# Attention by four-head groups with sinks padded to full tiles, between the matmuls of a token and channel mixer

## The chip, the cores and the metric

The kernel runs on one core of one Trainium2 chip. The metric is the device time of one execution in microseconds (us). Executions are sorted into fast and slow by their time (slow: over 1.5% above the fastest run of the same kernel). Medians and extremes that are quoted are of all runs, and the text says where slow ones are among them. The engines are called as in the profile: PE (TensorE matmuls), PEld (its weight loads), ACT (ScalarE), DVE (VectorE), POOL (GpSimd) and SP (SyncE, which here only issues DMAs).

## The reference, cut to what matters

Attention with 4 batches, 8 heads, 768 positions and 64 columns per head: each query sees a window of 128 keys and the first 4 keys ("sinks"). The heads are put side by side to x (4 x 768 x 512), which goes through an MLP mixer.

```python
keep = is_sink | ((rel >= 0) & (rel < window))          # n_sink = 4, window = 128
a = softmax(where(keep, q @ k.T / 8, -1e9)); x = heads_side_by_side(a @ v)
u = x + (relu(x.T @ w_tok1) @ w_tok2).T                 # 768 -> 256 -> 768
out = u + relu(u @ w_ch1) @ w_ch2                       # 512 -> 1536 -> 512
```

Inputs and output are fp32; both kernels compute in bf16.

## The kernel before: the parts that count

Two heads (one "pair") lie side by side in the 128 partitions, 64 rows each. A tile scheduler orders each engine's instructions. Scores are computed transposed (keys on partitions), one matmul of 64 rows at a time, each with its own exp on ACT and its own mask multiply on DVE or POOL. P·V (the exponentials of the scores, times the values) takes, for each head and query tile, the current key tile, the previous one, and the sinks, which are a matmul of **4 rows**.

```python
# loads: casting DMAs (fp32 in, bf16 out) of POOL's queue, six for each pair
nc.gpsimd.dma_start(out=qk_bf[:, 0, :, i], in_=q[b, h0 + i].rearrange("(t p) d -> p t d", p=P))
# scores
nc.tensor.matmul(ps_s[:, 0:nq * P], kT[:, kt], qT[:, kt:kt + nq], start=True, stop=True)       # 64 rows
nc.scalar.activation(pT[:, kt, i, 0:nq], ps_s[:, 0:nq * P], AF.Exp, scale=scale)
eng.tensor_tensor(out=pT[:, kt, i, 0:nq], in0=pT[:, kt, i, 0:nq], in1=msk[:, i, 0:nq], op=ALU.mult)
# ... sink scores
nc.tensor.matmul(ps_sk, kT2[ds(64 * i, 64), 0, 0:4], qT2[ds(64 * i, 64), 2:NT], start=True, stop=True)
# P.V of one head and one query tile
nc.tensor.matmul(ps_o, pT[:, qt, i, 0], vh[:, qt], start=True, stop=(qt == 0))                 # L149
nc.tensor.matmul(ps_o, pT[:, qt - 1, i, 1], vh[:, qt - 1], start=False, stop=(qt == 1))        # L151
nc.tensor.matmul(ps_o, pT_sink[:, i, ts(qt - 2, P)], vh[0:4, 0], start=False, stop=True)       # L153, 4 rows
# ... mixer of one batch: token product (L171, L182), transposes, channel products (L199, L208)
```

The mixer of batch b is spread between the attention of batch b+1.

The softmax here doesn't subtract the row's maximum and nothing guards it: scores larger than these inputs give would overflow.

## Time and profile before

Median 330.11 us (325.12 to 332.06, 4 runs, of which 331.77 and 332.06 are slow by the 1.5% rule); the profiled run spans 326.6 us.

The page of the kernel before, first its line of busy times (share of the span, instructions), then three of its lines of 40 equal slices of 8.2 us: the busy tenths of PE, the granted TensorE clock, and the busy tenths of the DMA engines.

```profile
PE 289.8 (89%) x1743; PEld 140.8 (43%) x1760; DVE 137.3 (42%) x491; ACT 164.2 (50%) x441; POOL 150.7 (46%) x215
...
PE   1584299899999999999999999999999999889994
...
PEclk9999999999999998999999999999959999999999
DMA  9999999999395773528379095313000002100022
```

PE is the busiest engine, and from 40 us on it is nearly always busy. What it is busy with is the question. The timeline of PE (start, duration in us, engine, line, operation, output and inputs, rows\*columns of the stationary operand, which PEld loads, then rows x columns of the moving one; the rows of both are the contraction rows, over which the matmul sums):

```profile
231.22 0.20 PE L149 MATMUL ps_o<-v_aug,pT 128*128 128x65 bf16 x1
231.26 0.20 PE L151 MATMUL ps_o<-v_aug,pT 128*128 128x65 bf16 x1
231.39 0.20 PE L153 MATMUL ps_o<-v_aug,pT_sink 4*128 4x65 bf16 x1
231.52 0.20 PE L149 MATMUL ps_o<-v_aug,pT 128*128 128x65 bf16 x1
...
232.46 0.34 PE L199 MATMUL ps_mx<-uT,w_ch_96 128*128 128x384 bf16 x1
232.73 0.28 PE L123 MATMUL ps_sc<-qT_2966,kT_2967 64*128 64x256 bf16 x1
232.94 0.20 PE L149 MATMUL ps_o<-v_aug,pT 128*128 128x65 bf16 x1
```

Matmuls overlap, so their durations are not to be added: read the distance from start to start. L149 to L151, both of 128 rows, is 0.04 us; L151 to L153, from 128 rows to 4, is 0.13 us, and so is the way back. A 384-column matmul that is followed by another of its kind takes 0.162 us (median of all in the trace); before a matmul of 64 rows it takes 0.27. Each change of the number of contraction rows costs about 0.1 us. Counted through all PE matmuls in order of time, there are 551 such changes.

The table of stages (start:end, length, then busy us and number of instructions of each engine, granted clock, share of DMA, which adds up the packets' times and can exceed 1, GB/s) has as its borders the first matmul of each batch's mixer. The first stage is the attention of batch 0 alone, three stages mix batch b's mixer with batch b+1's attention, and the last is the last mixer alone.

```profile
0.00:66.90 66.90, 41.30 (x238) 19.51 (x239) 24.57 (x103) 33.33 (x91) 54.62 (x81) 1.00 1.23 116
66.90:145.40 78.50, 76.31 (x463) 36.87 (x467) 37.10 (x136) 42.51 (x120) 43.22 (x59) 0.98 0.67 58
145.40:213.80 68.40, 67.14 (x438) 33.19 (x441) 34.79 (x123) 40.32 (x110) 36.28 (x50) 1.00 0.61 59
213.80:280.60 66.80, 65.41 (x401) 31.75 (x403) 30.12 (x112) 35.09 (x95) 14.38 (x22) 0.95 0.11 27
280.60:327.00 46.40, 39.67 (x214) 19.44 (x215) 10.69 (x19) 12.98 (x26) 2.18 (x4) 1.00 0.11 40
```

The mixed batches are bound by PE: the second busiest engine, ACT, has 40 of 68 us. The first of them is 10 us longer than the next. Its matmuls tell why; the timeline at the first mixer:

```profile
66.93 1.46 PE L171 MATMUL ps_mx<-x_sb_98,w_tok_94 128*128 128x512 bf16 x3
```

Three matmuls of 512 columns start 0.40 to 0.43 us apart; after 88 us the same shape steps 0.216 us. Two rows of another matmul of 512 columns, on either side of 88 us:

```profile
85.98 1.06 PE L182 MATMUL ps_mx<-h1T,w_tok_95 128*128 128x512 bf16 x2
...
88.81 0.59 PE L182 MATMUL ps_mx<-h1T,w_tok_95 128*128 128x512 bf16 x2
```

PE runs at half clock until then. The line PEclk does not show it: the first clock record of the packed trace begins at 87.6 us (no view prints it), and where there is no record the line shows full clock. Two shorter stretches at half clock are on record, 3.4 us from 128.6 us and 6.8 us from 237.8 us.

### The profile page before, as it was taken

The numbers are of one execution on the slowest core, as the hardware profiler recorded it, in microseconds if no ns is written. First come the engines' busy times: TensorE is split into PE (matmuls) and PEld (weight loads), VectorE is DVE, ScalarE is ACT, GpSimd is POOL, SyncE is SP. The second block draws the span as 40 slices with busy tenths as digits, with TensorE's granted clock in tenths as the row PEclk, the third lists the DMA queues.
The fourth block names the chain that finished last, engine by engine and source line by source line (L and its number), as shares of the span: only waits on it lengthen the run. The fifth ranks groups of instructions, "written<-read, shape, count | busy, mean of one in ns | idle before, by whom it ended". The sixth has DMA issues, their size and how long they took to land.

```text
span 326.6 us, 4967 instructions
## 1 busy us (share of the span) xinstructions
PE 289.8 (89%) x1743; PEld 140.8 (43%) x1760; DVE 137.3 (42%) x491; ACT 164.2 (50%) x441; POOL 150.7 (46%) x215
## 2 busy tenths in 40 slices
PE   1584299899999999999999999999999999889994
PEld 1221244333455554444545544444544454345541
DVE  1342155635763525237853335258614242350021
ACT  1374167756367887018378774063768730137400
POOL 8986559988375774217477455043223100000001
PEclk9999999999999998999999999999959999999999
DMA  9999999999395773528379095313000002100022
GB/s 71 90 183 206 173 64 73 76 58 72 26 61 38 50 49 25 88 101 78 24 54 71 3 61 66 101 63 27 0 2 0 1 19 101 75 2 0 2 96 96
DMA packets 82072, 19.98 MB, mean 61 GB/s; under 512 B 75808, under 2 KB 79136, under 8 KB 82048
## 3 DMA queue, kind: packets, MB, share of 16 engines
q0 software_dynamic: 79024, 15.34, 54.2%
q1 hardware_dynamic: 1728, 2.36, 1.9%
q10 hardware_dynamic: 1296, 1.97, 1.6%
q8 instruction: 14, 0.23, 0.3%
q14 instruction: 10, 0.08, 0.1%
HBM read 26.74 MB, written 6.29 MB: 101 GB/s over the span
## 4 chain that ended last, share of the span: by engine, by line
PE 54%; issue 22%; POOL 8%; DMA 7%; DVE 4%; ACT 4%; POOLq 0%; ACTq 0%
PE ps_mx L199 14%; PE ps_mx L208 10%; PE ps_sc L123 9%; DMA qk_bf<-in_k_dram 6%; PE ps_o L149 5%; PE ps_o L153 4%; PE ps_mx L171 3%; DVE u_sb L186 2%; POOL qk_bf L94 2%; POOL pT L131 2%; PE ps_sc L138 2%; PE ps_tr L108 2%; ACT pT L127 2%; PE ps_mx L182 1%; PE ps_tr L107 1%
## 5 line engine op out<-in xcount | busy, mean ns | idle before, releaser
L127 ACT ACTIVATE pT<-ps_sc 128x256 bf16<-128x256 f32 x192 | 66.5, 368 | 30.2 <-PE ps_sc L123 26.2
L199 PE MATMUL ps_mx<-uT,w_ch_96 128*128 128x384 bf16 x384 | 80.6, 332 | 0.7 <-DVE uT L190 0.5
L208 PE MATMUL ps_mx<-w_ch_97,v1T 128*128 128x512 bf16 x278 | 67.1, 384 | 0.4
L203 ACT ACTIVATE v1T<-ps_mx 128x384 bf16<-128x384 f32 x96 | 46.6, 489 | 35.0 <-PE ps_mx L199 34.8
L131 POOL TENSOR_TENSOR pT<-pT,mask_main 128x256 bf16<-128x256 bf16 (+1 forms) x80 | 50.2, 634 | 23.9 <-ACT pT L127 21.8
L154 DVE RECIPROCAL recip<-ps_o 128x1 f32<-128x1 f32 x192 | 29.8, 164 | 66.8 <-PE ps_o L153 40.7
L199 PEld LDWEIGHTS <-w_ch_96 128*128 128x128 bf16 x384 | 35.0, 98 | 25.5 <-issue 6.6
L222 POOL DMA_DIRECT2D out_dram<-o_sb x7 | 4.0, 574 | 81.8 <-DVE o_sb L213 81.8
L208 PEld LDWEIGHTS <-v1T 128*128 128x128 bf16 x288 | 27.6, 98 | 32.1 <-issue 1.8
L213 DVE TENSOR_TENSOR o_sb<-ps_mx,u_sb 128x512 f32<-128x512 f32 x24 | 16.6, 691 | 58.6 <-PE ps_mx L208 58.6
L149 PE MATMUL ps_o<-v_aug,pT 128*128 128x65 bf16 x192 | 37.1, 212 | 3.1 <-DVE x_sb_98 L160 1.1
L98 POOL DMA_DIRECT2D v_aug<-in_v_dram x32 | 27.4, 861 | 22.8 <-PE ps_tr L107 7.8
L131 DVE TENSOR_TENSOR pT<-pT,mask_main 128x256 bf16<-128x256 bf16 (+1 forms) x80 | 34.4, 431 | 7.9 <-ACT pT L127 7.4
L94 POOL DMA_DIRECT2D qk_bf<-in_q_dram x32 | 27.4, 859 | 17.4 <-PE ps_o L149 7.1
L107 PE MATMUL ps_tr<-ident,qk_bf 128*128 128x128 bf16 x96 | 15.2, 257 | 20.1 <-DMA qk_bf<-in_q_dram 12.9
L151 PE MATMUL ps_o<-v_aug,pT 128*128 128x65 bf16 x160 | 32.6, 211 | 0.0
L149 PEld LDWEIGHTS <-pT 128*128 128x128 bf16 x192 | 18.6, 102 | 24.3 <-issue 11.6
L96 POOL DMA_DIRECT2D qk_bf<-in_k_dram x32 | 27.2, 859 | 0.2 <-issue 0.2
L153 PE MATMUL ps_o<-v_aug,pT_sink 4*128 4x65 bf16 x128 | 26.8, 209 | 0.0
L131 POOL TENSOR_TENSOR pT<-pT,mask_first 128x256 bf16<-128x256 bf16 x16 | 11.0, 686 | 19.9 <-ACT pT L127 19.9
L139 ACT ACTIVATE pT_sink<-ps_sc 4x512 bf16<-4x512 f32 x32 | 17.9, 582 | 4.4 <-PE ps_sc L138 4.0
L107 PEld LDWEIGHTS <-qk_bf 128*128 128x128 bf16 x96 | 8.8, 110 | 23.0 <-issue 12.2
(142 smaller groups left out, 313.9 us busy)
## 6 DMA issues: line engine op xcount, KB each, us to landing
qk_bf<-in_q_dram POOLq DMA_DIRECT2D x32, 96.0 KB, 3.1
qk_bf<-in_k_dram POOLq DMA_DIRECT2D x32, 96.0 KB, 3.3
v_aug<-in_v_dram POOLq DMA_DIRECT2D x32, 96.0 KB, 3.4
out_dram<-o_sb SPq DMA_DIRECT2D x8, 256.0 KB, 2.0
out_dram<-o_sb ACTq DMA_DIRECT2D x7, 256.0 KB, 2.0
out_dram<-o_sb POOLq DMA_DIRECT2D x7, 256.0 KB, 2.3
w_ch_96<-in_moe_w_ch_dram POOLq DMA_DIRECT2D x1, 1536.0 KB, 12.5
w_ch_97<-in_moe_w_ch_dram POOLq DMA_DIRECT2D x1, 1536.0 KB, 15.1
```

The lines of the kernel that those rows point to most:

```text
L94: nc.gpsimd.dma_start(out=qk_bf[:, 0, :, i], in_=q[b, h0 + i].rearrange("(t p) d -> p t d", p=P))
L98: nc.gpsimd.dma_start(out=v_aug[:, i, :, 0:D], in_=v[b, h0 + i].rearrange("(t p) d -> p t d", p=P))
L123: nc.tensor.matmul(ps_s[:, 0:nq * P], kT[:, kt], qT[:, kt:kt + nq], start=True, stop=True,)
L127: nc.scalar.activation(pT[:, kt, i, 0:nq], ps_s[:, 0:nq * P], AF.Exp, scale=scale,)
L131: eng.tensor_tensor(out=pT[:, kt, i, 0:nq], in0=pT[:, kt, i, 0:nq], in1=msk[:, i, 0:nq], op=ALU.mult,)
L149: nc.tensor.matmul(ps_o, pT[:, qt, i, 0], vh[:, qt], start=True, stop=(qt == 0))
L151: nc.tensor.matmul(ps_o, pT[:, qt - 1, i, 1], vh[:, qt - 1], start=False, stop=(qt == 1))
L153: nc.tensor.matmul(ps_o, pT_sink[:, i, ts(qt - 2, P)], vh[0:4, 0], start=False, stop=True)
L154: nc.vector.reciprocal(recip[:, i], ps_o[:, D:D + 1])
L199: nc.tensor.matmul(ps_v1, w_ch1[:, ct, ts(ft, P)], uT[:, ct, ds(half * (S // 2), S // 2)], start=(ct == 0), stop=(ct == NC - 1),)
L203: nc.scalar.activation(v1T[:, ft, ds(half * (S // 2), S // 2)], ps_v1, AF.Relu)
L208: nc.tensor.matmul(ps_out, v1T[:, ft, ts(st, P)], w_ch2[:, ft], start=(ft == 0), stop=(ft == NF - 1),)
```

## The change

The intent: fewer and larger instructions. Four heads form a group. Scores come in units of four matmuls of 64 rows with one wide exp; masks become selects on POOL (instructions that zero what lies outside the window), but for the first tile; loads are plain fp32 DMAs of SP, cast on chip; the sink operands are padded to 128 rows, so that P·V has one sink matmul of 260 columns for four heads; and PE's order is set by hand, with the attention of batch b+1 spread between the pieces of batch b's mixer.

```diff
+        nc.sync.dma_start(out=q32.rearrange("p h t d -> p h (t d)"),
+                          in_=q[b, h0:h0 + GH].rearrange("h (p t) d -> p h (t d)", t=NT))
+        ...                                              # k alike, v in 256-byte pieces; casts on POOL
+        ps = ps_sc.tile([P, 2, 512], FP32, name="ps_s", tag="sc")
+        for kt in (2 * u, 2 * u + 1):
+            for i in range(2):
+                nc.tensor.matmul(ps[:, i, n:n + w], G.kT[j][ds(64 * i, 64), ts(kt, P)],
+                                 G.qT[j][ds(64 * i, 64), ds(kt * P, w)], start=True, stop=True)
+        nc.scalar.activation(pT[:, :, 512 * u:512 * u + n], ps[:, :, 0:n], AF.Exp, scale=scale)
-                    nc.tensor.matmul(ps_o, pT_sink[:, i, ts(qt - 2, P)], vh[0:4, 0], start=False, stop=True)
+                nc.tensor.matmul(ps, G.pk[:, ts(qt - 2, P)], vsink[:, g], ...)     # 128 rows, four heads
+    with tc.manual_schedule(engines={PE}):
+        ...
+            main = a + m + c1 + c2
+            fill = batch_attention(b + 1) if b + 1 < B else []
+            run(spread(main, fill, 0.05, 0.92))
```

## The prediction

> **What bounds the kernel now.** TensorE. On the page it is busy 89% of 326.6 us; ACT has 50%, POOL 46%, DVE 42%, and these overlap it. But much of that is not arithmetic:
>
> 1. *Tile-size switches.* In the timeline, successive 128-row 512- and 384-column matmuls start 216 and 162 ns apart. Where a 64-row score matmul follows they are 323 and 268 ns apart; a 65-column P·V matmul takes about 30 ns, but 129 ns before a 4-row sink matmul, and 131 ns after one. Each change of contraction rows thus costs about 105 ns. The Trainium skill, "TensorEngine Tiling (Array Packing)", Key Properties, says changing the tiling mode drains TensorE; this trace agrees and gives the size. I count 551 changes in the order of the matmuls: about 55 us.
> 2. *Half clock.* Until about 88 us a 512-column matmul steps 401 to 427 ns, then 216; the granted-clock line does not show it. "TensorE: Matmul & The Clock Gate", Part 1, has these two rates. From 40 to 88 us PE is busy, at half rate.
> 3. *Start.* 30–40 us is nearly empty: the chain of waits has 15.3 us for a k load behind the weight loads (casting DMAs). The first mixer matmul is at 67 us.
>
> **What the change does.**
> - Sinks: 128 four-row matmuls become 24 full-height ones of 260 columns, and score matmuls for sinks become full height. No 4-row switches remain.
> - Scores run in 48 units of four 64-row matmuls: about 96 switches, not 551. Saves about 48 us.
> - Fp32 loads by the SP queue, and casts on chip: POOL loses some 85 us of DMA issue (0.86 us each) and DMA work halves or better; it gains casts and masks (estimate from its 128x256 multiply, 0.68 us, and 128x128 select, 0.33 us: about 28 us per batch). ACT gets wide exps: by its 385 ns for 256 and 594 ns for 512 columns, 1.0 us for 1024; about 29 us per batch. DVE about 25 us.
> - PE order is fixed, so a late exp or mask now stalls everything behind it.
>
> **Sum (estimates from the steps above).** PE per mixer: 24 x 216 + 24 x 56 + 96 x 162 + 72 x 216 ns = 37.7 us. Attention per batch: transposes 2.7, scores with switches 5, sinks 0.9, P·V 3.8: 12.3 us. PE total about 200 us.
> Start (attention of batch 0 alone, bound by loads, exps and POOL masks, not PE): 38 us. Three mixed batches: 3 x 50, plus 5 us each of stalls (VectorE in token mixing, ScalarE in the first channel matmul). Last mixer 40. Half clock after the start 4, throttle 2, output 3. Total 252 us; the run times lie 2 to 5 us over the span, so I name **254 us**, range **237 to 282**. Nearly all of the PE saving lies on the critical path because PE is the bound from 40 us on. Chances: faster 0.96, same 0.02, slower 0.02.
>
> **What would show it.** PE busy about 80–88% of a shorter span; no 4-row matmuls; switches near 100; the first mixer matmul near 38–42 us; 216/162 ns steps soon afterwards; POOL under 65% with no DMA issues but weights; ACT waits on scores, not PE on ACT; the last mixer about 40 us as before.
>
> **What would make it wrong.** POOL slower than estimated (strided fp32 casts, selects of 512–640 columns, or waiting on VectorE's copies), so fixed-order PE stalls each batch; a start over 50 us because fp32 loads and 7.9 MB of weights share the DMA engines; PE staying at half clock well into the first mixed batch; transposed PSUM copies (strided bf16) much slower than 0.9 us.

## The result, and the profile after

Median 263.91 us (263.84 to 264.61, 4 runs), against 330.11 us. A ratio here is the mean time of one kernel's fast runs over that of the other's of the same rounds, so it is not quite the ratio of the medians that are quoted: 0.8081, with a 95% interval of 0.8007 to 0.8154 (the fast runs of the kernel before are 325.12 and 328.45 us). The page of the kernel after, the same lines:

```profile
PE 213.8 (82%) x1648; PEld 115.0 (44%) x1648; DVE 107.2 (41%) x202; ACT 115.6 (44%) x193; POOL 88.7 (34%) x143
...
PE   0532061787899999978999999888999998999994
...
PEclk9999996779999999999999999999999999999999
DMA  6999999998936117710000122100000122000132
```

PE, among mixer and attention matmuls in a mixed batch, in the timeline:

```profile
133.84 0.39 PE L192 MATMUL ps_s<-qT,kT 64*128 64x256 bf16 x4
134.16 0.82 PE L274 MATMUL ps_v<-uT,w_ch_103 128*128 128x384 bf16 x4
134.82 0.28 PE L228 MATMUL ps_o<-va,pT 128*128 128x65 bf16 x4
```

Four score matmuls go through in 0.32 us, because two of 64 rows, for the two heads of a pair, start 3 to 4 ns apart. (The Trainium skill, "TensorE: Matmul & The Clock Gate", Part 3, describes such concurrent row tiles; this trace agrees, with the 3 to 4 ns.) The whole execution has 86 changes of the number of rows. The stages, with their borders again at the first matmul of each mixer:

```profile
0.00:55.00 55.00, 20.91 (x196) 13.26 (x197) 25.04 (x44) 19.32 (x23) 31.71 (x53) 0.91 1.07 260
55.00:109.20 54.20, 51.14 (x417) 27.46 (x415) 24.71 (x49) 26.63 (x46) 25.22 (x38) 1.00 0.58 169
109.20:163.10 53.90, 50.93 (x413) 27.38 (x412) 24.30 (x48) 26.56 (x46) 20.43 (x32) 1.00 0.13 45
163.10:217.10 54.00, 51.03 (x414) 27.43 (x413) 24.35 (x48) 26.56 (x46) 11.29 (x20) 1.00 0.08 30
217.10:262.10 45.00, 39.77 (x217) 19.51 (x215) 8.82 (x13) 16.54 (x32) 0.00 (x0) 1.00 0.11 42
```

With the changes counted in each stage, at 105 ns each:

| stage | before, us | after, us | saved | changes before / after | their share of the saving |
|---|---|---|---|---|---|
| attention of batch 0 | 66.9 | 55.0 | 11.9 | 112 / 14 | not on the path: PE mostly waits |
| first mixed batch | 78.5 | 54.2 | 24.3 | 159 / 24 | 14.2 |
| second mixed batch | 68.4 | 53.9 | 14.5 | 150 / 24 | 13.2 |
| third mixed batch | 66.8 | 54.0 | 12.8 | 130 / 24 | 11.1 |
| last mixer | 46.4 | 45.0 | 1.4 | 0 / 0 | 0 |

The changes account for 38.5 of the 51.6 us saved in the mixed batches. Of the other 10 us of the first batch I put most down to the half clock before, which lasted for 24.1 us of it: its longer steps add up to some 8.6 us (each matmul's columns at the half-clock and the full-clock step), and those of the 6.8 us in the third batch to 2.9. In the kernel after, the first mixer matmuls run at full clock, as its timeline shows.

```profile
55.05 2.92 PE L256 MATMUL ps_h<-x_b,w_tok_101 128*128 128x512 bf16 x12
```

The first of the twelve steps 0.385 us, the others 0.216, where it was 0.40 to 0.43 us.

What is left is two small effects of opposite sign. Pairs of score matmuls that go through side by side save about 0.11 us each (an estimate: 256 columns at the step of 0.216 us for 512); there are 24 in each mixed batch, against 3 to 10 before, so some 2 us. And PE is idle for 3.0 us of each mixed batch, where it was for 1.3 to 2.2 us. The side-by-side pairs come with the same edit as the fewer changes, and no run parts the two. Nor does a run show which part of the change brings the 11.9 us of the start; the loads and casts alone (e7) brought none of it.

The start is the stage that I had predicted worst: 55.0 us, not 38. Its DMA issues of SP in the timeline, two lines of the DMA view (queue, operation, KB, us from issue to landing), and the sink values:

```profile
1.84 0.50 SPq L85 DMA_DIRECT2D v_109<-in_v_dram  x1
2.38 15.81 SPq L81 DMA_DIRECT2D q_129<-in_q_dram  x1
18.23 2.74 SPq L83 DMA_DIRECT2D k_130<-in_k_dram  x1
...
v_109<-in_v_dram SPq DMA_DIRECT2D x1, 768.0 KB, 20.6
q_129<-in_q_dram SPq DMA_DIRECT2D x1, 768.0 KB, 22.0
...
38.50 6.22 POOL L128 TENSOR_SCALAR vsink<-vs_c,dm 16x512 bf16<-16x512 f32 x4
...
44.77 0.38 PE L224 MATMUL ps_o<-vsink,pk 128*128 128x260 bf16 x1 [5.24 <-POOL vsink L128]
```

v of the first group takes 20.6 us to land, and q of the second 22.0; SP hangs 15.8 us in the issue of the latter. POOL had issued three weight loads in the first 5 us: they depend on nothing, so the scheduler took them to the front. Later, PE waits 5.24 us for POOL's sink values.

### The profile page after: what moved, and what is told of

The parts are those of the page before. It is cut to its first block, busy times and chain, and to the rows that moved or that the text cites. A ratio compares the mean times of both kernels' runs of the same rounds, so it can differ in the third digit from the quotient of the medians.

```text
span 262.1 us, 4072 instructions
## 1 busy us (share of the span) xinstructions
PE 213.8 (82%) x1648; PEld 115.0 (44%) x1648; DVE 107.2 (41%) x202; ACT 115.6 (44%) x193; POOL 88.7 (34%) x143
## 2 busy tenths in 40 slices
DMA packets 40051, 29.40 MB, mean 112 GB/s; under 512 B 25568, under 2 KB 36576, under 8 KB 40032
## 4 chain that ended last, share of the span: by engine, by line
PE 65%; DVE 9%; DMA 8%; ACT 6%; POOL 5%; issue 4%; SPq 1%; ACTq 0%; DVEq 0%; POOLq 0%
PE ps_w L283 24%; PE ps_v L274 23%; DMA q_129<-in_q_dram 8%; PE ps_h L256 4%; ACT pT L198 3%; PE ps_s L192 3%; PE ps_tr L168 3%; DVE kT L174 3%; DVE u_sb L263 2%; DVE pT L200 2%; PE ps_o L228 2%; PE ps_o L232 2%; POOL vsink L128 2%; ACT uT L269 1%; DVE qT L174 1%
## 5 line engine op out<-in xcount | busy, mean ns | idle before, releaser
L274 PE MATMUL ps_v<-uT,w_ch_103 128*128 128x384 bf16 x384 | 72.6, 326 | 2.2 <-ACT v_514 L276 0.7
L198 ACT ACTIVATE pT<-ps_s 128x1024 bf16<-128x1024 f32 (+1 forms) x48 | 45.3, 964 | 12.6 <-PE ps_s L192 12.6
L207 POOL TENSOR_SCALAR_AFFINE_SELECT pT<-pT 128x640 bf16<-128x640 bf16 x32 | 24.0, 752 | 45.5 <-ACT pT L198 45.5
L286 DVE TENSOR_TENSOR o<-ps_w,u_sb 128x512 f32<-128x512 f32 x24 | 16.6, 692 | 47.4 <-PE ps_w L283 47.4
L269 ACT ACTIVATE uT<-ps_ut 128x512 bf16<-128x512 bf16 x24 | 14.5, 606 | 17.8 <-PE ps_ut L268 17.6
L192 PE MATMUL ps_s<-qT,kT 64*128 64x256 bf16 x192 | 19.9, 292 | 2.3 <-ACT pT L198 1.9
L236 DVE TENSOR_TENSOR x_b<-ps_o,rc 128x256 bf16<-128x256 f32 x48 | 20.4, 424 | 1.6
L263 DVE TENSOR_TENSOR u_sb<-ps_u,x_b 128x512 bf16<-128x512 f32 x24 | 15.8, 684 | 12.6 <-PE ps_u L262 12.6
L228 PE MATMUL ps_o<-va,pT 128*128 128x65 bf16 x192 | 19.3, 203 | 1.5 <-POOL pT L207 1.1
L210 POOL TENSOR_SCALAR_AFFINE_SELECT pT<-pT 128x512 bf16<-128x512 bf16 x32 | 20.5, 640 | 0.0
L283 PE MATMUL ps_w<-w_ch_104,v_1191 128*128 128x512 bf16 x72 | 17.3, 379 | 0.0
L283 PE MATMUL ps_w<-w_ch_104,v_514 128*128 128x512 bf16 x72 | 17.3, 379 | 0.0
L283 PE MATMUL ps_w<-w_ch_104,v_1868 128*128 128x512 bf16 x72 | 17.3, 379 | 0.0
L232 PE MATMUL ps_o<-va,pT 128*128 128x65 bf16 x160 | 16.8, 203 | 0.0
L283 PE MATMUL ps_w<-w_ch_104,v_2533 128*128 128x512 bf16 x72 | 15.7, 379 | 0.0
## 6 DMA issues: line engine op xcount, KB each, us to landing
v_109<-in_v_dram SPq DMA_DIRECT2D x1, 768.0 KB, 20.6
```

The costliest lines, as they stand in the source:

```text
L192: nc.tensor.matmul(ps[:, i, n:n + w], G.kT[j][ds(64 * i, 64), ts(kt, P)], G.qT[j][ds(64 * i, 64), ds(kt * P, w)], start=True, stop=True)
L198: nc.scalar.activation(pT[:, :, 512 * u:512 * u + n], ps[:, :, 0:n], AF.Exp, scale=scale)
L207: nc.gpsimd.affine_select(out=cur, in_=cur, compare_op=ALU.is_ge, fill=0.0, base=0, pattern=[[0, NT - 1], [1, P]], channel_multiplier=-1)
L210: nc.gpsimd.affine_select(out=prv, in_=prv, compare_op=ALU.is_ge, fill=0.0, base=-1, pattern=[[0, NT - 2], [-1, P]], channel_multiplier=1)
L228: nc.tensor.matmul(ps[:, h], pT[:, i, ds(256 * qt, P)], G.va[:, h, qt], start=(qt < 2 and h == 0), stop=(h == GH - 1 and qt == 0), skip_gr ...
L232: nc.tensor.matmul(ps[:, h], pT[:, i, ds(256 * (qt - 1) + P, P)], G.va[:, h, qt - 1], start=False, stop=(h == GH - 1), skip_group_check=True)
```

## The experiments

Theory A: the gain of the mixed batches is the cost of the changes of rows. Rival B: it is the lighter work of POOL and ACT and the other loads. Rival C: it is the hand-set order as such. For the start, theory D says that it is bound by the loads, rival P by POOL. The first numbers of each measurement are the median and the extremes of its runs. All kernels gave correct results. The kernel before was run again with each set of experiments, the kernel after was not, and the sets ran on different chips; so differences to the kernel after are across rounds. That its later mixed batches, untouched there, take the same 53.9 us in e4, e5, e6 and e8 speaks for comparing them.

### e1: the kernel before with full-height sinks alone

```diff
-        pT_sink = pt_pool.tile([4, 2, (NT - 2) * P], BF16, name="pT_sink")
+        pT_sink = pt_pool.tile([P, 2, (NT - 2) * P], BF16, name="pT_sink")
-            nc.tensor.matmul(ps_sk, kT2[ds(64 * i, 64), 0, 0:4], ...)
+            nc.tensor.matmul(ps_sk, kT2[ds(64 * i, 64), 0], ...)
-                    nc.tensor.matmul(ps_o, pT_sink[:, i, ts(qt - 2, P)], vh[0:4, 0], ...)
+                    nc.tensor.matmul(ps_o, pT_sink[:, i, ts(qt - 2, P)], v_sink[:, i], ...)   # zero from row 4 on
```

> The kernel before with one part of the change alone: the 128 sink matmuls of P.V get 128 rows (the sink scores of all 128 keys of the first tile are taken, and the value rows beyond the 4 sinks are zero). Nothing else is changed: loads, masks, order by the scheduler. Theory A (the gain of the mixed batches is the cost of changing the number of contraction rows, about 105 ns each): of 551 changes some 213 go, so 20 to 22 us less, 330 to about 309 us (306 to 314), and the matmuls that follow one another at 65 columns are 30 to 40 ns apart where they were 129. Rival B (the gain is the lighter POOL and ACT work and the loads) and rival C (the gain is the hand-set order as such, with fewer waits): within 3 us of 330.

Measured: 307.5 us (306.73 to 309.09), ratio 0.9344 (0.9255 to 0.9433). The changes fell from 551 to 340; 211 x 105 ns are 22.2 us. The kernel before has a median of 330.38 us in these rounds, but of 327.54 without its two slow runs, so the difference of fast medians is 20.0 us. The timeline of P·V, with the sink matmul at L157, then the second mixed batch (68.40 us in the kernel before):

```profile
152.60 0.19 PE L153 MATMUL ps_o<-v_aug,pT 128*128 128x65 bf16 x1
152.63 0.19 PE L155 MATMUL ps_o<-v_aug,pT 128*128 128x65 bf16 x1
152.66 0.19 PE L157 MATMUL ps_o<-v_sink,pT_sink 128*128 128x65 bf16 x1
152.69 0.49 PE L203 MATMUL ps_mx<-uT,w_ch 128*128 128x384 bf16 x2
...
136.10:200.70 64.60, 62.18 (x445) 30.21 (x443) 36.89 (x131) 39.33 (x110) 36.12 (x50) 1.00 0.65 62
```

The sink matmul now starts 0.03 us after the one before it, where it was 0.13. Padding 4 rows to 128 makes PE do more arithmetic in the same number of instructions, and the program is faster. Theory A holds in direction; loads, masks and the ordering by the scheduler were not touched. That the total agrees so well with 22.2 us is in part luck. In the second mixed batch, at full clock in both, 56 fewer changes are worth 5.9 us, and 3.8 were gained, mostly because PE waits more: its idle time there rose from 1.3 to 2.4 us. And in the profiled runs the mixed batches of the kernel before had 30.9 us at half clock and those of e1 10.7, which by the longer steps is some 6.6 of the 21.3 us between their spans.

### e2: the kernel after with the padding undone

```diff
-                nc.tensor.matmul(ps, G.pk[:, ts(qt - 2, P)], vsink[:, g], ...)
+                nc.tensor.matmul(ps, G.pk[0:4 * GH, ts(qt - 2, P)], vsink[0:4 * GH, g], ...)
```

> The kernel after, with the padding of the sink operands alone undone: the 32 sink matmuls read 16 rows of the same tiles, not 128. Theory A: 64 more changes of contraction rows at 105 ns, 6.7 us, of which 48 (5.0 us) lie in the mixed batches, which PE bounds: 264 to 269 us, or up to 270.5 us; each mixed batch from 54.0 to 55.7 us. Rivals B and C: no difference, 264 us within 1.

Measured: 270.4 us (269.95 to 270.88), 6.5 us over the kernel after. The changes are 146, 60 more (four sink matmuls follow a 64-row one, where there was a change already): 6.3 us at 105 ns. The second and third mixed batch take 55.55 us each, at full clock as in the kernel after:

```profile
112.07:167.62 55.55, 52.58 (x414) 26.69 (x413) 24.28 (x48) 26.56 (x46) 20.44 (x32) 1.00 0.13 43
```

That is 1.6 us more for 16 more changes, 102 ns each. Theory A again, and here neither clock nor waits are mixed in.

### e8: the cost by itself, in two twins

```diff
                 nc.tensor.matmul(ps, v1[:, ft, ts(st, P)], w_ch2[:, ft], ...)
+                if b == B - 1:
+                    tiny = ps_sc.tile([P, 2, 512], FP32, name="ps_s", tag="sc")
+                    nc.tensor.matmul(tiny[:, 0, 0:64], ident[0:64], ident[0:64, 0:64], start=True, stop=True)
```

The twin reads `ident[0:128]`.

> The cost by itself: the kernel after, with a tiny matmul of 64 rows and 64 columns of the identity (result unused) behind each of the 72 matmuls of the last mixer's second channel product, where PE is bound by nothing else. Theory A: 144 changes, so 72 x (2 x 105 + 30) ns = 17 us more: 264 to 281 us, and the stretch from its first to its last matmul from 15.3 to about 32.6 us. Rival (it is the additional matmul or its weight load that costs, not the change of rows): the same as the twin run with 128 rows.

> The control of the twin run: the same 72 tiny matmuls with 128 rows, so no change of the number of rows. Theory A: 72 x 30 ns = 2.2 us more: 266 us, stretch about 17.5 us. Rival (the additional matmul or its weight load costs): the same as the twin, 281 us.

Measured in the same rounds: 281.51 us (280.99 to 281.62) with 64 rows, 266.36 us (266.04 to 266.64) with 128. The timeline of the twin with 64 rows, then of that with 128:

```profile
250.01 0.20 PE L286 MATMUL ps_s<-ident 64*128 64x64 bf16 x1
250.15 0.39 PE L283 MATMUL ps_w<-w_ch,v 128*128 128x512 bf16 x1
250.47 0.20 PE L286 MATMUL ps_s<-ident 64*128 64x64 bf16 x1
```

```profile
250.04 0.19 PE L286 MATMUL ps_s<-ident 128*128 128x64 bf16 x1
250.06 0.38 PE L283 MATMUL ps_w<-w_ch,v 128*128 128x512 bf16 x1
250.28 0.19 PE L286 MATMUL ps_s<-ident 128*128 128x64 bf16 x1
```

From one tiny matmul to the next it is 0.46 us with 64 rows and 0.24 with 128. From the first matmul of the stretch to the last tiny one it is 32.6 against 17.6 us, with 143 changes against none: 15.0 us / 143 = 105 ns. The matmul itself costs next to nothing; changing the number of rows does. A matmul of half the rows makes the program slower.

### e3: the kernel after without the hand-set order

```diff
-    with tc.manual_schedule(engines={PE}):
+    if True:
```

> The kernel after, with the scheduler's own order on TensorE in place of the hand-set one; all instructions are the same. Theory A (the order is worth what it saves in changes of contraction rows): the changes rise from 86 to 150 or more, and the mixed batches grow by 105 ns for each additional one, time 270 to 285 us. Rival C (the hand-set order saves waits): the mixed batches have gaps of several us where PE waits, at about the same number of changes. If neither order nor count differs: 264 us.

Measured: 262.28 us (261.89 to 263.83), ratio to before 0.7935 (0.7873 to 0.7996). My expectation missed: PE's order differs in many places, but the changes are 88, nearly as few as with 86, and the later mixed batches are 53.1 us, even a little shorter. The hand-set order is worth nothing here. The scheduler keeps the score units together of its own accord; the units themselves (four matmuls into one tile, one exp), and the sink scores, which e1 left at 64 rows, are what is left to account for the 254 changes between e1's 340 and the 86. That part was not tried alone.

### e7: the kernel before with the fp32 loads and casts alone

```diff
-            nc.gpsimd.dma_start(out=qk_bf[:, 0, :, i], in_=q[b, h0 + i].rearrange("(t p) d -> p t d", p=P))
+            f = stage.tile([P, NT, D], FP32, name=f"q32{i}")
+            nc.sync.dma_start(out=f, in_=q[b, h0 + i].rearrange("(t p) d -> p t d", p=P))
+            nc.gpsimd.tensor_copy(out=qk_bf[:, 0, :, i], in_=f)                    # k and v alike
```

> The kernel before, with one part of the change alone: q, k and v come as fp32 by the SP queue and are cast by POOL (layout of the loads as before). POOL loses some 82 us of DMA issue and gains 96 casts of 384 columns (about 0.5 us each, from 0.83 us for 768 columns in the kernel after: 48 us). Theory A: the mixed batches, bound by PE and its changes of rows, keep 66 to 69 us; only the start changes, where a k load was waited for 15.3 us: 318 to 330 us. Rival B (the loads and POOL carry the gain): below 305 us, and mixed batches below 62 us.

Measured: 336.41 us (334.5 to 339.19), ratio 1.0189 (1.009 to 1.0288): a little slower, which neither theory had. POOL's busy time fell from 150.7 to 115.8 us, and nothing was gained, so rival B falls for loads and POOL. ACT's share of it, the wide exps, was not tried alone; but PE was idle for only 1.3 to 2.2 us of each mixed batch of the kernel before, and lighter work elsewhere could return little more than that. The start did not improve either (first mixer at 68.2 us, not 66.9): transposes now wait for POOL's casts. The second and third mixed batch, 72.1 and 70.6 us, are nearly 4 us longer; their granted clock is 0.93 and 0.88, where it was 1.00 and 0.95:

```profile
146.60:218.70 72.10, 71.36 (x443) 34.20 (x441) 34.25 (x123) 40.38 (x110) 27.60 (x50) 0.93 0.24 61
218.70:289.30 70.60, 69.77 (x406) 32.59 (x404) 30.22 (x112) 35.23 (x95) 13.51 (x22) 0.88 0.06 23
```

By the longer steps the clock makes up some 4 us in each, so that at equal clock these batches take as long as before, which is what theory A had. Why the clock dropped more often was not found out.

### e4: the kernel after with late weights

```diff
     def load_weights():
+        q1, v1 = first_loads                     # of the second head group
+        for w, src in ((w_tok1, q1), (w_tok2, q1), (w_ch1, v1), (w_ch2, v1)):
+            nc.gpsimd.tensor_copy(out=w[0:1, 0, 0:1], in_=src[0:1, 0, 0, 0:1])
```

The copied element is overwritten by the load, which therefore has to wait for the copy.

> My prediction had the first mixer start at 38 us; it starts at 55 us. The kernel after, with the four casting weight loads held back by a one-element copy each, until q (token weights) and v (channel weights) of the second head group have landed. Theory D (the start is bound by the DMA engines: the weight loads, issued in the first 4 us, delay v of group 0 and q, k, v of group 1, which land at 22, 24, 26 and 29 us): these land near 11, 13, 16 and 18 us, and the first mixer matmul comes 8 to 11 us earlier, 44 to 47 us; time 253 to 256 us. Rival P (the start is bound by POOL: selects, casts and the 6.2 us of sink values): the loads land earlier, but the first mixer stays within 3 us of 55, time 261 to 264 us. The mixed batches stay at 54.0 us in both.

Measured: 255.34 us (253.09 to 257.16, the last slow), ratio to before 0.7706 (0.7624 to 0.7788). The second group's q is cast from 12.81 us on (24.42 in the kernel after), and the first mixer matmul comes at 44.2 us. SP's issue of that load takes 5.65 us and not 15.81. Theory D: the weights had been taking the DMA engines from the loads that PE needed first. The Trainium skill, "DMA: Bandwidth & Descriptors", Queues, rings and completion order, says that each DMA engine goes round-robin between the queues that have work; that loads of one queue slow those of another is what this pair of runs shows: that q was issued at 2.38 us in both, and could be used at 24.42 or at 12.81 us.

### e5: the kernel after with early sinks

The four small sink loads are issued by ACT ahead of group 1's loads, and the two instructions of the loop that makes `vsink` use `nc.vector` and not `nc.gpsimd`.

> The kernel after, with the sink value loads issued by the ACT queue before group 1's loads, and the sink values masked on VectorE and not on POOL. In the kernel after, POOL spends 38.5 to 44.7 us on them, and the sink matmul waits 5.2 us for that. Theory P (POOL bounds the start): 4 to 6 us earlier, time 258 to 260 us, first mixer at 49 to 51 us. Theory D alone (only the loads' landing counts): less than 2 us, 262 us or more.

Measured: 261.64 us (261.32 to 262.1), first mixer at 51.9 us. The time is between the two theories' numbers: the 5.24 us wait of PE is only partly on the path as long as the loads come late.

### e6 and e11: both edits of the start, in the hand-set and in the scheduler's order

> The kernel after with both edits of its start: weights held back until group 1's q and v have landed, and the sink values loaded early and masked on VectorE. With the late weights alone the first mixer came at 44.2 us, and TensorE had waited 8.7 us (from 23.7 to 32.4 us) for a POOL that was at the sink values (25.4 to 31.6 us). Theory D then P (the loads bound the start, and behind them POOL): 5 to 8 us less than with late weights alone, 247 to 250 us, first mixer at 36 to 39 us. Rival (the sink values are covered by other waits, as they mostly were where they were moved alone, 2.3 us): 253 to 255 us.

> The same with the scheduler's own order on TensorE. In the kernel after that order cost nothing: mixed batches of 53.1 us, not 54.0, at 88 changes of contraction rows. If order is worth nothing in itself: within 2 us of the run with both edits and the hand-set order, 246 to 250 us. Rival (hand-set order pays where the start is not bound by loads): 3 us or more slower.

Measured: e6 252.81 us (250.84 to 257.31, one of four runs slow), ratio to before 0.7645 (0.7475 to 0.7815); e11 249.52 us (249.33 to 250.47). Two stages of e6, the start and the first mixed batch:

```profile
0.00:34.20 34.20, 19.58 (x195) 12.67 (x198) 23.38 (x52) 19.10 (x23) 23.42 (x47) 0.99 1.07 276
34.20:97.10 62.90, 54.74 (x411) 29.06 (x415) 23.91 (x49) 26.78 (x46) 27.37 (x41) 0.92 0.82 224
```

The first mixer comes at 34.2 us, 10 us earlier than in e4 and more than I had expected, but the first mixed batch gives 9 us of them back: 62.9 us, not 54. So the time missed the 247 to 250 us. The clock has a part in this: it is at half for 9.6 us of that batch (0.92), worth some 4 us of longer steps. The timeline of POOL has it waiting 5.10 us for a load of v and 4.04 us for one of k, and PE waits 4.36 us behind POOL. The DMA engines were full until about 68 us. e11 is 2.3 us below the fast median of e6, so the hand-set order brings nothing here either.

### e12: the last weights later still

```diff
             nc.vector.tensor_tensor(out=u_sb[:, st], in0=ps, in1=x_b[:, st], op=ALU.add)
+            if b == 0 and st == 0:
+                nc.gpsimd.tensor_copy(out=w_ch2[0:1, 0, 0:1], in_=u_sb[0:1, 0, 0:1])
+                nc.gpsimd.dma_start(out=w_ch2, in_=moe_w_ch2.rearrange("(t p) n -> p t n", p=P))
```

> With both edits of the start the first mixer came at 34.2 us (28.6 in the scheduler's order), but the first mixed batch took 62.9 us (68.0), not 54: POOL waited for the loads of groups 2 and 3, TensorE for POOL, and the DMA engines were full until about 68 us. Theory F (the DMA engines' work of the first 65 us is the floor, and what counts is which load comes first): the both-edits kernel in the scheduler's order, with the second channel weights (3.1 MB in HBM, not needed until some 65 us) held back until the first tile of u of the first mixer is there, some 40 us. Groups 2 and 3 land earlier, the first mixed batch takes 55 to 60 us and not 68.0, time 238 to 243 us. Rival (the wait is POOL's own order, not the loads): first mixed batch 66 us or more, time 247 to 251 us. If the weights come too late instead, the second channel product starts with a wait for them.

Measured: 241.06 us (240.35 to 241.32), ratio to before 0.7299 (0.721 to 0.7388). The first two stages:

```profile
0.00:31.00 31.00, 15.07 (x151) 9.59 (x153) 21.81 (x44) 18.99 (x23) 18.14 (x39) 0.89 1.07 294
31.00:87.50 56.50, 53.40 (x451) 29.21 (x457) 26.56 (x57) 26.57 (x46) 33.03 (x49) 1.00 0.99 255
```

The first mixed batch is back at 56.5 us, where e11, with the same order, took 68.0. (Of these 11.5 us some 2 are the half clock that e11 had there and e12 has not; the rest is waits of PE.) Theory F holds: in these two stages the DMA engines are the scarce thing (their share is 1.07 and 0.99), and the order of the loads decides. This is the fastest version: 23 us below the kernel after, and it does not need the hand-set order.

### e10: warming the clock, without a result

Twenty dummy matmuls were added at the head of the first mixer of the kernel before.

> The part of the gain that I put down to TensorE's half clock. The kernel before, with 20 dense dummy matmuls of 512 columns (result unused) at the head of the first mixer, at 67 us, where TensorE runs at half clock until 88 us. Theory H (the clock is late because the work until then is too sparse; once granted, it mostly stays): full clock within 8 us of the first dummy, the rest of the first mixed batch as fast as its successors: 78.5 us become about 69 to 70 us and the dummies' 5 to 8.5 us, so the total moves little, 326 to 331 us. Rival (the kind of work, with its many changes of rows, holds the clock down in this batch): half clock again soon after the dummies, the batch 78 us and the dummies on top, 336 to 340 us.

Measured: 331.09 us (326.57 to 333.58; two of four runs slow, the profiled one too), ratio 0.9936 (0.9738 to 1.0134). The experiment missed its aim: nothing held the dummies in place, and the scheduler ran them at 8.5 to 23.8 us, in the start. It does not say what dense work at 67 us would have done. But its clock records begin early enough to show the half clock: full for 3.4 us from 23.5 us, then half until 91.8 us, through the first 23 us of the first mixed batch, although PE was busy for 95% of them:

```profile
68.80:91.80 23.00, 21.87 (x105) 9.37 (x106) 13.05 (x46) 10.89 (x33) 15.01 (x21) 0.50 0.81 52
```

So what the half clock cost is read from the steps of the matmuls in the traces, and no experiment removed it alone; why the clock stays low until 88 us in the kernel before, and is full from 55.4 us on in the kernel after, is open.

## Why the prediction was right

The measured 263.91 us lie within the range of 237 to 282, 4% over the 254 named. Point by point:

- *What bounds the kernel before, changes of rows:* right, and shown three ways. The size of 105 ns was confirmed by the twins (15.0 us for 143 changes) and by e2 (6.5 us for 6.3 computed); e1 moved by 20.0 us for 22.2, with clock and waits mixed in. I predicted about 96 changes, and there are 86 (and 24 full-height sink matmuls, where there are 32).
- *A mixed batch of 50 us of PE work plus 5 us of stalls:* 54.2, 53.9 and 54.0 us, of which PE is busy for 51 and idle for 3.
- *The last mixer as before:* 45.0 us with its output, against 43 in the sum (40 + 3).
- *Start, 38 us:* wrong, 55.0 us. This is the term that was mis-sized, by 17 us. I had named it as a risk ("fp32 loads and 7.9 MB of weights share the DMA engines"), but in the sum I let the loads land as if the weights came later, because the program lists them later. They depend on nothing, and were issued first. e4 brought the first mixer to 44.2 us, and e6, with POOL relieved as well, to 34.2.
- *Half clock for 4 us after the start, 2 us of throttling:* neither came; the first mixer ran at full clock but for its first 0.35 us, and no later record within the span is below it. These made up 6 of the 17 us.
- *The sum:* 252 us, against a span of 262.1. The start is 17.0 us over, the last mixer 2.0; the mixed batches are 2.9 under, the clock terms 6.0. That the total is within 4% is in part luck: errors of opposite sign.
- *"PE order is fixed, so a late exp or mask now stalls everything behind it":* no such stall of weight; and the order as such is worth nothing (e3), which I had not considered.
- *DMA work "halves or better":* not quite; it fell by 44%, from 58% of 326.6 us to 41% of 262.1 (sum of the queues' shares), although the bytes that were moved rose from 19.98 to 29.40 MB.

## What to carry to other kernels

On a busy TensorE, count the changes of the number of contraction rows in order of time: each cost 105 ns here, half of a matmul of 512 columns. Pad a short operand with zeros to full height, and keep the matmuls of 64 rows together; their order as such mattered little. A load that depends on nothing may be issued first whatever its place in the program: give large, late-needed weights a dependency, so that they do not take the DMA engines from what is needed first.

## What the Trainium skill lacked or had wrong

- "TensorEngine Tiling (Array Packing)", Key Properties, says that changing the tiling mode drains TensorE, without a cost: 105 ns per change between 128 and 64 rows at full clock (15.0 us for 143 changes), 102 ns with 16 rows (e2) and about 100 with 4.
- "TensorE: Matmul & The Clock Gate", Back-to-back issue gap, gives 131 ns per matmul of 512 columns and 81 ns for 128 columns as the sustained spacing in real kernels. Here they are 216 ns, and 56 ns for the transposes of 128 columns, at full clock, which is that page's formula for the isolated gap.
- The same page, Part 4, says that full clock does not engage for transposes. Transposes of 128 columns step 56 ns in the full-clock stages, and 107 ns in the half-clock stage, as other matmuls do. Whether transposes alone would bring the clock up no run here shows.
- The same page, Part 1, has the full clock after about 3.4 us of sustained work. In the kernel before, PE was 90 to 95% busy from 40 to 80 us, and the first grant of full clock on record is at 87.6 us; in e10 it was 95% busy for 23 us with half clock on record. No page says how dense the work must be.
- "GPSIMD Engine Reference", Engine selection, has one-input work at roughly line rate on GpSimd. Multiplying 16 x 512 fp32 elements by a scalar for each partition took 1564 ns on POOL and 470 ns on VectorE (e6). A cast of 128 x 768 elements from fp32 came nearer, 0.83 us on POOL and 0.56 on VectorE (e4).
- No page says that in a profile without an early clock record the granted clock reads as full: the kernel before shows 1.00 for its first stage, where matmuls stepped at half rate.
